# First layer of three batches instead of four in seven products, and all row sums on VectorE

## The chip, the core and the metric

The kernel runs on one core of one Trainium2 chip. The metric is device time in microseconds (us) for one execution, as the median of several runs. TensorE (PE) does the matmuls, VectorE (DVE), ScalarE (ACT) and GpSimd (POOL) the elementwise work, SyncE (SP) only issues DMAs here.[...]

## The reference

Attention without a softmax is followed by a two-layer network with an exact GELU. The outputs of the heads stand side by side as the network's input rows, so that 8 x 448 rows of 768 numbers go through it.

```python
# q, k, v: (8, 12, 448, 64) f32; w_in (768, 2048), w_out (2048, 768)
scores = scale * np.matmul(q, k.transpose(0, 1, 3, 2))      # scale = 1/sqrt(64)
attn = np.maximum(scores, 0.0) ** 2 / S                     # S = 448
attn_out = np.matmul(attn, v)
x = attn_out.transpose(0, 2, 1, 3).reshape(B * S, H * D)    # (3584, 768)
h = x @ w_in
g = 0.5 * h * (1.0 + erf(h * inv_sqrt2))
return g @ w_out
```

## The kernel before, in words

Everything is computed in bf16 with f32 sums. The attention of the eight batches runs one batch after the other, in three groups of four heads. For each group there are seven steps: score matmuls into PSUM (`ps`, L663), a relu with scale from PSUM to the bf16 tile `a_sq` on ACT (L675) or DVE (L677), and its square on DVE (L684, one tile multiplied by itself). When the seven squares of a group are there, the value product (`pav`, L724) follows and is copied to the transposed input `xT` (L440 on DVE or L442 on ACT). Queries and keys have to stand transposed (`qT`, `kT`). From batch 2 on, DMA transposes on SP's queue do this, nine for each batch (L589). POOL issues the loads of the inputs and, between them, small copies called gates (L630), each of which waits for the transposes of a group of heads before the next load overwrites their source.

While the attention of a batch runs, PE takes matmuls of the network in between, from a list called `flow`. The first layer of batches 0 to 3 is computed directly (`add_f1`, `psh`, L776): sixteen blocks of output columns, six matmuls of 448 columns each, and a GELU from PSUM on ACT (L786). The first layer of batches 4 to 7 is computed by `add_blocks`: input, weights and output are each cut into two by two blocks and seven products take the place of eight. It makes 168 matmuls of 224 columns for a batch (`pb`, L924), needs four sums of input blocks on DVE (`xs`, L890), sums of weight blocks (`ws`, L846, once for all batches) and 20 additions on DVE that pass partial results on (`part`, L958). These products come last, after the last score matmul, in the list called `end`; this part is called the tail below.

The second layer is computed for fourteen groups of 256 rows each (`add_group`, `pso`, L1095) by seven products too. The right-hand sums of `w_out` are made once (`t_sb`, L1031). Each group needs four sums of its own rows (`s_sb`, L1075), 128 x 1024 in bf16 each. For groups 2 to 6 these four stand in POOL's queue, placed by the table `POOLED` behind the gates and loads of the batch that it names; for the other groups they are on DVE. After each product DVE or ACT passes the partial result on (L1129, L440, L442), and SP issues the output stores (L1055), in the same queue as the transposes. Groups 1 to 6 stand in `flow` (table `GROUPS`), the later ones in `end`, partly woven with the blocks.

The order of instructions on each engine is written when the program is built. A planner (`Scheduler`) holds a price for each operation (for example 0.69 us for a row sum on DVE, 2.3 on POOL) and places operation after operation; the opening follows a fixed list (`ORDER`), PE's later work follows `pe_q`, POOL's follows `pool_q`. ACT and DVE take what the planner judges due, and a relu can go to either. `F1B` names, for each batch of attention, the batch whose direct first layer is put into `flow`; `SHARES` spreads `flow` over the batches.

Of the kernel before, what the change touches and what calls it, by code (L numbers as in the profile page):

```python
# [12 lines left out]
B, H, S, D = 8, 12, 448, 64  # L13
# [13 lines left out]
KF = FF // 128  # L27
# [27 lines left out]
SUM_BIAS = -0.3  # L55
TSUM_BIAS = 0.2
LEADS = {}
POOLED = {2: 3, 3: 3, 4: 5, 5: 5, 6: 5}
SHARES = (1.3, 1.0, 1.0, 1.0, 1.0, 1.0)
LAST = 256  # L60
PASSES = 5
# [262 lines left out]
def kernel(  # L324
# [9 lines left out]
    nc = tc.nc  # L334
# [101 lines left out]
    V, A = nc.vector, nc.scalar  # L436
# [7 lines left out]
    def e_copy(n, psum=4):  # L444
# [4 lines left out]
    sch = Scheduler({"w": 3, "a": NA, "f": 2, "osb": 3, "s1": 1, "s2": 1, "s3": 1, "s4": 1,  # L449
                     "p": 1})  # L450
    pool_q, pe_q = [], []
# [9 lines left out]
    QK, SQ, AV, X, GL = {}, {}, {}, {}, {}  # L461
    F1, F2 = {}, {}
# [27 lines left out]
    def add_v(b, g0, g1):  # L490
        def fn():
            get_v(b)
            nc.gpsimd.dma_start(vt[b][:, 2 * g0 : 2 * g1], kv_view(v, b, g0, g1))

        old = [o for (bb, *_), o in AV.items() if bb == (b - 2 if b == B - 1 else b - 3)]
        o = dma(fn, (g1 - g0) * 4 * S * 256, old)
        for g in range(g0, g1):
            ld_v[b, g] = [o]

    def add_load(b, g0=0, g1=G):  # L500
        add_k(b, g0, g1)
        add_q(b, g0, g1)
        if b < 3:
            add_v(b, g0, g1)
# [120 lines left out]
    def add_gate(b, g):  # L625


        def fn(e):
            n = (16 * g + 1) * KC
            nc.gpsimd.tensor_copy(gate, get_T(b)[0][:, n : n + 16 * KC : KC])  # L630

        deps = [Tq[b, g, c][0] for c in range(NC)] + [Tk[b, g, 0][0]]
        pool_q.append(sch.add((("POOL", 0.2, 0.3),), fn, deps))
# [174 lines left out]
    def wpart(i, j, m0=0, m1=M1):  # L808
        return win_sb[:, i * K1 : i * K1 + K1, (j * M1 + m0) * 128 : (j * M1 + m1) * 128]
# [19 lines left out]
    def wcols(n, m0, m1):  # L829
        t, m = wtile(n, m0)  # L830
        return t[:, :, 128 * m : 128 * (m + m1 - m0)]

    WS = {}
    blocks = {}

    def add_wsums(after, done):

        last = [o[0] for (bb, *_), o in list(Tq.items()) + list(Tk.items()) if bb == B - 1]
        last += [o for (bb, *_), o in QK.items() if bb == B - 2]
        add, sub = mybir.AluOpType.add, mybir.AluOpType.subtract  # L840

        def one(n, m0, op, a, b, deps):
            m1 = m0 + M1 // 2
            return sch.add(
                (("DVE", 0.95, 1.07),),
                lambda e: V.tensor_tensor(wcols(n, m0, m1), a(m0, m1), b(m0, m1), op=op),  # L846
                deps + last + after,
            )

        def part(i, j):  # L850
            return lambda m0, m1: wpart(i, j, m0, m1)

        def summed(n):
            return lambda m0, m1: wcols(n, m0, m1)

        for m0 in (0, M1 // 2):
            s1 = one(1, m0, add, part(0, 1), part(1, 1), [])
            s2 = one(2, m0, sub, summed(1), part(0, 0), [s1])
            s4 = one(4, m0, sub, part(1, 0), summed(2), [s2])
            s3 = one(3, m0, sub, part(0, 0), part(0, 1), [s1] + done)  # L860
            WS[m0] = {1: s1, 2: s2, 3: s3, 4: s4}

    def add_blocks(b):


        xs = [o for (bb, g, h), v in X.items() if bb == b for o in v]
        box = {}
        add, sub = mybir.AluOpType.add, mybir.AluOpType.subtract
        half = (slice(0, HS), slice(HS, S))

        def x(i, c):
            return lambda: xT[b][:, i * K1 : i * K1 + K1, half[c]]

        def t(n):
            def fn():
                if "t" not in box:
                    tag = "qT" if b == B - 1 else "kT"
                    box["t"] = tpool.tile([128, 4, K1, HS], BF16, tag=tag, name="xs")
                return box["t"][:, n - 1]

            return fn

        gone = [o for (bb, *_), o in QK.items() if bb == (B - 2 if b == B - 4 else B - 1)]
        if b == B - 2:
            gone += blocks[B - 4]

        def xsum(n, op, l, r, deps):
            return sch.add(
                (("DVE", 0.47, 0.58),),
                lambda e: V.tensor_tensor(t(n)(), l(), r(), op=op), deps + xs + gone,  # L890
            )

        t1 = xsum(1, sub, x(0, 1), x(0, 0), [])
        t2 = xsum(2, sub, x(1, 1), t(1), [t1])
        t3 = xsum(3, sub, x(1, 1), x(0, 1), [])
        t4 = xsum(4, sub, x(1, 0), t(2), [t2])
        TS = {1: t1, 2: t2, 3: t3, 4: t4}
        old = readers.get(b - 2, [])
        atoms = []
        for m4 in (0, M1 // 2):  # L900
            bank, todo = {}, []
            for y in range(2):
                ms = range(m4 + 2 * y, m4 + 2 * y + 2)
                todo.append(add_block(b, m4, y, ms, bank, x, t, TS, xs, old, half))
            for p in zip(*todo):
                atoms += [(0.58, o) for o in p]
                blocks.setdefault(b, []).extend(p)
            for name in ("a", "b", "c"):
                u, v = bank["end", name]
                u.joint, v.joint = [v], [u]  # L910
        return atoms
# [143 lines left out]
            queue.pop(0).dma_start(to[k, p0 : p0 + m, c], src[y : y + m, c])  # L1055
            j += m

    def add_group(g, pooled=None):

        rows = [range(256 * g + 128 * x, 256 * g + 128 * x + 128) for x in range(2)]  # L1060
        bs = sorted({r // S for t in rows for r in (t[0], t[-1])})
# [8 lines left out]
        box = {}  # L1070

        def sum_op(n, op, a, b, deps):
            def fn(e):
                box["s", n] = spool.tile([128, K2, 128], BF16, tag=f"s{n}", name=f"s{n}_sb")
                (V if pooled is None else nc.gpsimd).tensor_tensor(box["s", n], a(), b(), op=op)  # L1075

            eng = ("DVE", 0.69, 0.8) if pooled is None else ("POOL", 2.3, 2.5)
            o = sch.add((eng,), fn, deps, need=(f"s{n}",), bias=SUM_BIAS)
            if pooled is not None:
                pooled.append(o)  # L1080
            mine.append(o)
            return o

# [131 lines left out]
    def f1(b):  # L1215
        return [(1.14, add_f1(b, m)) for m in range(KF)]

    def steps(b):
        return [((b, g, i, None),) for g in range(G) for i in range(NK)]
# [54 lines left out]
    def early(eng, get, src, t):  # L1274
        def fn(e):
            get_nat(0)
            copy(e, get(), src)

        n = src.shape[1] * src.shape[2]
        d = 0.07 + n / 960 if eng == "DVE" else 0.12 + 0.00074 * n  # L1280
        return sch.add(((eng, d, d + 0.12),), fn, [landed(t)])

    o = early("ACT", lambda: nq[0][:, :4, : HC * D], q32, 5.3)
# [4 lines left out]
    for eng, i0, i1 in (("DVE", 0, K_CUT), ("ACT", K_CUT, NK)):  # L1288
        c = slice(i0 * D, i1 * D)
        o = early(eng, lambda c=c: nk[0][:, :2, c], k32[:, :, c], 5.45)  # L1290
# [54 lines left out]
    def at(b, n):  # L1345
        return [at_slot(b, n)]
# [1 line left out]
    for g in range(G):  # L1348
        add_load(3, g, g + 1)
    add_v(3, 0, G)  # L1350
    flow, plans, held = [], {}, {}
    F1B = {2: 1, 3: 2, 4: 3}
    GROUPS = {2: (1,), 3: (2, 3), 4: (4, 5), 5: (6,)}
    for b in range(2, B):
        add_steps(steps(b), dve=True)
        if b == 2:
            x1 = f1(1)
            first_atoms = x1[:LEAD]
            flow += x1[LEAD:]
            flow += [(2.6, add_plain(t, n)) for n in (1, 0) for t in (0, 1)]  # L1360
            add_tsums()
        elif b in F1B:
            flow += f1(F1B[b])
        if b + 1 < B:

            n = {2: 2}.get(b, 1)
            add_T_dma(b + 1, [at(b, n + y // 3) for y in range(9)])
            if b + 2 < B:
                for g in range(G):
                    add_gate(b + 1, g)  # L1370
                    add_load(b + 2, g, g + 1)
                add_v(b + 2, 0, G)
        flow += [y for g in GROUPS.get(b, ()) for y in add_group(g, held.setdefault(g, []) if g in POOLED else None)]
        for g in POOLED:
            if g in held and POOLED[g] == b:
                pool_q.extend(held[g])
    add_wsums(at(B - 1, 1), [F1[B - 5, m, None] for m in range(KF)])

    def woven(x, y):


        out, y = [], list(y)
        for n, o in enumerate(x):
            out.append(o)
            if n % 14 in (3, 9):
                out.append(y.pop(0))
        return out + y

    end = list(add_blocks(B - 4))
    end += woven(add_blocks(B - 3), add_group(7))  # L1390
    end += add_group(8)
    end += woven(add_blocks(B - 2), add_group(9))
    g10 = add_group(10)
    end += g10 + woven(add_blocks(B - 1), add_group(11))
    end += add_group(12) + add_group(13)
    pe_q.extend(x[1] for x in first_atoms)
    total, gone, edge = sum(x[0] for x in flow), 0.0, 0.0
# [50 lines left out]
```

## Time and profile before

| | |
|---|---|
| median of 3 runs | 401.08 us (397.18 to 409.08) |
| the profiled execution | 401.08 us, its span 399.3 us |
| PE busy | 366.6 us (92% of the span), 3629 matmuls |
| DVE busy | 305.4 us (76%) |
| ACT busy | 204.3 us (51%) |
| POOL busy | 110.2 us (28%) |
| attention of batches 2 to 7 | from 65.0 to 260.6 us of the span |
| tail, from the last score matmul | 260.6 to 399.3 us |

A stretch is bound by the engine that is busy throughout it. Where no engine is, one looks for the wait that ends last and for what released it. PE's clock is granted in shares, 1.00 being full speed[...]. In lines of the profile, `a<-b,c` names the tile written and the tiles read, and `xN` the number of instructions in the line. Batches, groups of heads and groups of rows are counted from 0.

### The profile page before, as it was taken

The page shows a single profiled execution, that of the slowest core. Times are in us where ns is not written, and L with a number is a line of the kernel's source. Part 1 is how long each engine was busy: PE and PEld are TensorE (multiplying, and loading weights), DVE is VectorE, ACT ScalarE, POOL GpSimd, SP SyncE. Part 2 cuts the span into 40 slices and gives each one's busy share as a digit, 9 for nine tenths or more (in the row PEclk, how much of TensorE's full clock was granted, in tenths as well). Part 3 has the DMA queues.
Part 4 walks back from the last instruction along what each step waited for, and adds up shares of the span by engine and source line. Part 5 has one row for each costly group of instructions (what it writes and reads, how often), then busy time and mean ns, then how long its engine had stood idle before and what let it go on. Part 6 is the DMA issues. An engine that isn't in the chain of part 4 may idle for free.

```text
span 399.3 us, 8659 instructions
## 1 busy us (share of the span) xinstructions
PE 366.6 (92%) x3629; PEld 231.3 (58%) x3629; DVE 305.4 (76%) x484; ACT 204.3 (51%) x316; POOL 110.2 (28%) x123
## 2 busy tenths in 40 slices
PE   8699999999999839799979879899999999999995
PEld 7476554455544315354425434469997698689663
DVE  3999814898987708998799979998979766765862
ACT  5988855755587605347745516655553145025300
POOL 8755212401123096901390817200000000000000
PEclk9999999999999969899989969999999999999999
DMA  9999999999999999599996111100201300220232
GB/s 177 194 204 203 202 172 171 203 196 163 194 222 174 162 161 130 119 178 212 189 207 93 41 39 42 39 2 18 65 2 34 97 30 2 80 79 2 71 88 80
DMA packets 89270, 47.28 MB, mean 118 GB/s; under 512 B 55312, under 2 KB 85776, under 8 KB 89232
## 3 DMA queue, kind: packets, MB, share of 16 engines
q0 software_dynamic: 32912, 22.47, 39.4%
q1 hardware_dynamic: 55952, 23.76, 32.5%
q8 instruction: 28, 0.46, 0.5%
q10 hardware_dynamic: 368, 0.51, 0.3%
q14 instruction: 10, 0.08, 0.1%
HBM read 45.61 MB, written 11.01 MB: 142 GB/s over the span
## 4 chain that ended last, share of the span: by engine, by line
PE 66%; DVE 15%; SPq 6%; ACT 5%; DMA 4%; issue 2%; POOL 2%; DVEq 0%; POOLq 0%; ACTq 0%
PE pso L1095 24%; PE pb L924 14%; PE psh L776 14%; DVE a_sq L684 8%; SPq L589 6%; PE ps L663 6%; PE pav L724 5%; DMA qT<-nq 4%; ACT a_sq L675 4%; DVE part L958 2%; DVE osb L1129 1%; DVE a_sq L677 1%; PE spin L1256 1%; DVE ws L846 1%; POOL s_sb L1075 1%
## 5 line engine op out<-in xcount | busy, mean ns | idle before, releaser
L675 ACT ACTIVATE a_sq<-ps 128x896 bf16<-128x896 f32 x131 | 113.4, 918 | 59.6 <-PE ps L663 59.4
L684 DVE TENSOR_TENSOR a_sq<-a_sq 128x896 bf16<-128x896 bf16 (+1 forms) x169 | 116.8, 733 | 3.0 <-ACT a_sq L675 2.3
L776 PE MATMUL psh<-xT,win_sb 128*128 128x448 bf16 (+1 forms) x420 | 77.9, 339 | 0.0
L1095 PEld LDWEIGHTS <-s_sb 128*128 128x128 bf16 x424 | 41.4, 100 | 40.9 <-issue 9.4
L958 DVE TENSOR_TENSOR part<-pb,part 128x448 f32<-128x448 f32 x80 | 46.1, 620 | 22.2 <-PE pb L924 22.2
L776 PEld LDWEIGHTS <-win_sb 128*128 128x128 bf16 x420 | 39.1, 98 | 36.6 <-issue 9.1
L677 DVE TENSOR_SCALAR a_sq<-ps 128x896 bf16<-128x896 f32 (+1 forms) x38 | 40.8, 1075 | 22.9 <-PE ps L663 22.8
L663 PE MATMUL ps<-qT,kT 64*64 64x448 bf16 (+1 forms) x756 | 48.9, 341 | 5.2 <-ACT a_sq L675 2.0
L1095 PE MATMUL pso<-t_sb,s_sb 128*128 128x384 bf16 x208 | 41.5, 347 | 10.1 <-POOL s_sb L1075 8.4
L724 PE MATMUL pav<-a_sq,v_sb 64*64 64x448 bf16 (+1 forms) x756 | 39.2, 333 | 8.6 <-DVE a_sq L684 7.4
L786 ACT ACTIVATE h_sb<-psh 128x448 bf16<-128x448 f32 x64 | 35.0, 550 | 23.2 <-PE psh L776 23.1
L1095 PEld LDWEIGHTS <-h_sb 128*128 128x128 bf16 x312 | 30.6, 100 | 24.6 <-issue 6.7
L1095 PE MATMUL pso<-wout_sb,h_sb 128*128 128x384 bf16 x208 | 39.8, 336 | 2.3 <-DVE osb L1129 2.3
L967 ACT ACTIVATE h_sb<-part 128x448 bf16<-128x448 f32 x48 | 26.7, 578 | 25.4 <-DVE part L958 25.1
L924 PEld LDWEIGHTS <-win_sb 128*128 128x128 bf16 x384 | 36.9, 98 | 3.1 <-issue 1.1
L1095 PE MATMUL pso<-wout_sb,s_sb 128*128 128x384 bf16 (+2 forms) x216 | 38.1, 320 | 0.1
L1129 DVE TENSOR_TENSOR osb<-pso,p_sb 128x384 f32<-128x384 f32 x39 | 21.6, 554 | 18.9 <-issue 10.1
L663 PEld LDWEIGHTS <-kT 64*64 64x64 bf16 x756 | 18.9, 106 | 27.5 <-issue 18.9
L724 PEld LDWEIGHTS <-v_sb 64*64 64x64 bf16 x756 | 21.8, 107 | 21.7 <-issue 12.6
L1075 POOL TENSOR_TENSOR s_sb<-h_sb 128x1024 bf16<-128x1024 bf16 x10 | 23.5, 2350 | 26.9 <-PE pso L1095 26.8
L630 POOL COPY gate<-qT 128x16 bf16<-128x16 bf16 x15 | 4.0, 267 | 94.5 <-DMA qT<-nq 94.5
L924 PEld LDWEIGHTS <-ws 128*128 128x128 bf16 x288 | 27.6, 98 | 0.4 <-issue 0.4
(62 smaller groups left out, 347.9 us busy)
## 6 DMA issues: line engine op xcount, KB each, us to landing
nk<-in_k_dram POOLq DMA_DIRECT2D x23, 224.0 KB, 6.9
nq<-in_q_dram POOLq DMA_DIRECT2D x21, 224.0 KB, 8.5
v_sb<-in_v_dram POOLq DMA_DIRECT2D x5, 672.0 KB, 12.9
out_dram<-osb SPq DMA_DIRECT2D x8, 336.0 KB, 3.2
v_sb<-in_v_dram POOLq DMA_DIRECT2D x9, 224.0 KB, 8.2
out_dram<-osb SPq DMA_DIRECT2D x7, 288.0 KB, 2.8
out_dram<-osb SPq DMA_DIRECT2D x8, 240.0 KB, 3.1
win_sb<-in_moe_w_in_dram POOLq DMA_DIRECT2D x8, 192.0 KB, 8.5
```

The costliest lines, as they stand in the source:

```text
L663: nc.tensor.matmul(ps[64 * j : 64 * j + 64, e, x * w : x * w + w], kT[r, g, i * 128 + 64 * j : i * 128 + 64 * j + 64], moving, start=True, ...
L675: A.activation(ar, ps, AF.Relu, scale=c_att)
L677: V.tensor_scalar(ar, ps, c_att, 0.0, op0=mybir.AluOpType.mult, op1=mybir.AluOpType.max,)
L684: V.tensor_mul(box["a2"][:, :, :used], ar, ar)
L724: nc.tensor.matmul(pav[0][o2 : o2 + 64, e, :w], vt[b][r, 2 * g + e, bass.ts(i, D)], box["a2"][r, y, o : o + w], start=(i == 0), stop=(i == ...
L776: nc.tensor.matmul(ph[:, x * n : x * n + n], win_sb[:, kd, bass.ts(m + x, 128)], xT[b][:, kd, c], start=(kd == 0), stop=(kd == KD - 1),)
L786: A.activation(h_ring()[:, m : m + nm, o + c.start : o + c.stop], box[0][:, :S].rearrange("p (x n) -> p x n", x=nm), AF.Gelu,)
L924: nc.tensor.matmul(bank[name][:, y, z * HS : z * HS + HS], w[:, k, bass.ts(mm, 128)], right()[:, k], start=first and k == 0 and z == 0, st ...
L958: V.tensor_add(get(to), ps(name), get(other))
L967: A.activation(h_ring()[:, m : m + 2, o + half[c].start : o + half[c].stop], src().rearrange("p (x n) -> p x n", x=2), AF.Gelu,)
L1075: (V if pooled is None else nc.gpsimd).tensor_tensor(box["s", n], a(), b(), op=op)
L1095: nc.tensor.matmul(box[bank][:, n0:n1], left()[:, kf], right()[:, kf, n0:n1], start=bool(need) and kf == 0, stop=kf == K2 - 1, skip_group_ ...
```

## The change

The first layer of batch 4 is computed directly. It stands in `flow` with batch 5 (`F1B`), so its 96 matmuls of 448 columns and its sixteen GELUs fall beside attention. `add_blocks` is called for batches 5, 6 and 7 only, and group 7 is still woven with the blocks of batch 5. The sums of weight blocks, one of which is written over a part of `w_in`, wait for the direct first layer of batch 4 instead of batch 3. `POOLED` is gone: the twenty row sums of groups 2 to 6 are on DVE, priced like the others, and POOL's queue holds only gates and loads. The buffers of `add_blocks` no longer have to wait for a fourth batch. As the planner spreads a longer `flow` over the same batches, the network's matmuls stand at other places among those of attention, and so do the stores in SP's queue. The opening, up to batch 2 of attention, keeps its order.

```diff
-POOLED = {2: 3, 3: 3, 4: 5, 5: 5, 6: 5}
...
-        gone = [o for (bb, *_), o in QK.items() if bb == (B - 2 if b == B - 4 else B - 1)]
-        if b == B - 2:
-            gone += blocks[B - 4]
+        gone = [o for (bb, *_), o in QK.items() if bb == (B - 2 if b == B - 3 else B - 1)]
...
-    def add_group(g, pooled=None):
+    def add_group(g):
...
-                (V if pooled is None else nc.gpsimd).tensor_tensor(box["s", n], a(), b(), op=op)
-
-            eng = ("DVE", 0.69, 0.8) if pooled is None else ("POOL", 2.3, 2.5)
-            o = sch.add((eng,), fn, deps, need=(f"s{n}",), bias=SUM_BIAS)
-            if pooled is not None:
-                pooled.append(o)
+                V.tensor_tensor(box["s", n], a(), b(), op=op)
+
+            o = sch.add(
+                (("DVE", 0.69, 0.8),), fn, deps, need=(f"s{n}",), bias=SUM_BIAS
+            )
...
-    F1B = {2: 1, 3: 2, 4: 3}
+    F1B = {2: 1, 3: 2, 4: 3, 5: 4}
...
-        flow += [y for g in GROUPS.get(b, ()) for y in add_group(g, held.setdefault(g, []) if g in POOLED else None)]
-        for g in POOLED:
-            if g in held and POOLED[g] == b:
-                pool_q.extend(held[g])
-    add_wsums(at(B - 1, 1), [F1[B - 5, m, None] for m in range(KF)])
+        flow += [y for g in GROUPS.get(b, ()) for y in add_group(g)]
+    add_wsums(at(B - 1, 1), [F1[B - 4, m, None] for m in range(KF)])
...
-    end = list(add_blocks(B - 4))
-    end += woven(add_blocks(B - 3), add_group(7))
+    end = woven(add_blocks(B - 3), add_group(7))
     end += add_group(8)
```

More of the change, by code (lines that the diff above doesn't have):

```diff
@@ L833 @@
     WS = {}
-    blocks = {}
     def add_wsums(after, done):
@@ L906, in add_blocks @@
                 atoms += [(0.58, o) for o in p]
-                blocks.setdefault(b, []).extend(p)
             for name in ("a", "b", "c"):
@@ L1350 @@
     add_v(3, 0, G)
-    flow, plans, held = [], {}, {}
-    F1B = {2: 1, 3: 2, 4: 3}
+    flow, plans = [], {}
+    F1B = {2: 1, 3: 2, 4: 3, 5: 4}
     GROUPS = {2: (1,), 3: (2, 3), 4: (4, 5), 5: (6,)}
```

## The prediction

> **What bounds the kernel now.** I first cut the span at the first score matmul of each batch and read the busy time in each stretch; the whole-span shares (PE 92%, DVE 76%) hide that the batches differ. Columns: stretch, its length, then busy time of PE, PE weight loads, DVE, ACT and POOL, the granted clock, the DMA share and GB/s. The rows are the attention of batches 2 to 7, then what follows the last score matmul.
>
> ```profile
> 65.00:97.56 32.56, 31.92 (x278) 16.18 (x278) 28.50 (x42) 21.16 (x31) 5.33 (x8) 1.00 1.31 186
> 97.56:125.53 27.97, 27.08 (x268) 13.86 (x268) 22.94 (x36) 19.28 (x28) 5.84 (x10) 1.00 1.28 197
> 125.53:167.04 41.51, 30.12 (x270) 15.11 (x270) 27.88 (x38) 17.07 (x23) 26.86 (x24) 0.88 1.04 143
> 167.04:194.23 27.19, 27.19 (x269) 13.88 (x268) 23.71 (x39) 17.77 (x25) 5.21 (x10) 1.00 1.28 200
> 194.23:225.81 31.58, 28.80 (x270) 13.94 (x270) 28.58 (x35) 17.45 (x24) 17.43 (x12) 0.95 0.85 131
> 225.81:260.60 34.79, 28.20 (x257) 13.59 (x256) 31.91 (x42) 15.97 (x21) 15.20 (x7) 0.90 0.15 42
> 260.60:399.31 138.71, 133.55 (x1124) 105.40 (x1116) 99.81 (x177) 48.34 (x92) 0.00 (x0) 1.00 0.16 46
> ```
>
> Batches 2, 3 and 5 are PE bound: PE works nearly all the time at full clock. Batches 4, 6 and 7 hold about as many matmuls and take up to 14 us longer, with a lower clock. Those three are the ones with much POOL work. The timeline of batch 4 shows the largest hole (start, length, engine, line, idle before it and its releaser):
>
> ```profile
> 139.25 0.21 POOL L630 COPY gate<-qT 128x16 bf16<-128x16 bf16 x1 [9.24 <-DMA qT<-nq]
> ...
> 142.04 2.13 POOL L1075 TENSOR_TENSOR s_sb<-h_sb 128x1024 bf16<-128x1024 bf16 x1
> 144.26 2.11 POOL L1075 TENSOR_TENSOR s_sb<-s_sb,h_sb 128x1024 bf16<-128x1024 bf16 x1
> ...
> 146.42 2.74 PE L1095 MATMUL pso<-t_sb,s_sb 128*128 128x384 bf16 x8 [8.43 <-POOL s_sb L1075]
> ```
>
> The sums s_sb stand in POOL's queue behind a gate that waits for a transpose; PE waits 8.43 us for the second of them. The other two bad batches have no such hole. There I asked for the squares (L684) alone in the same stretches (length, DVE busy, clock, DMA):
>
> ```profile
> 97.56:125.53 27.97, 12.18 (x21) 1.00 1.28 197
> ...
> 125.53:167.04 41.51, 16.84 (x21) 0.88 1.04 143
> 167.04:194.23 27.19, 12.28 (x22) 1.00 1.28 200
> 194.23:225.81 31.58, 17.50 (x19) 0.95 0.85 131
> 225.81:260.60 34.79, 19.76 (x21) 0.90 0.15 42
> ```
>
> The same squares cost 12.2 us where POOL makes no sums and 16.8, 17.5 and 19.8 where it does. Three squares from 201.58 on take 6.01 us in the timeline beside POOL sums, against 1.69 for three beside none. So the excess is 4.6 + 5.3 + 7.6 = 17.5 us of DVE time, in batches where DVE is busy 28 to 32 us: there it becomes the bound.
>
> [...] The trace shows 0.66 over 140 to 150 us, behind the 8.43 us hole, and 1.00 over both stretches beside it, so that a hole costs a little more than its length.
>
> **The change part by part.** Rates are from the chain of waits, where runs of one kind follow each other:
>
> ```profile
> 182.01 3.51 PE psh L776 x18
> ...
> 290.78 4.60 PE pb L924 x48
> 295.38 1.30 PE pso L1095 x8
> ```
>
> This is 0.195 us per first-layer matmul of 448 columns, 0.0958 per block matmul of 224, 0.163 per second-layer matmul. Scores come to 0.0615 and values to 0.0475 each from the same chain (12 in 0.69 to 0.76, 28 in 1.32).
>
> (1) Batch 4's first layer leaves the seven-product blocks. The tail loses 168 block matmuls, 168 x 0.0958 = 16.1 us. The attention phase gains 96 matmuls, 96 x 0.195 = 18.7 us. PE alone: +2.6 us. Both parts lie on the path, as PE is the bound in the tail and in the good batches.
>
> (2) With the instruction order of the two builds and these rates, PE's own work in batches 2 to 7 is 32.0, 27.3, 26.7, 27.4, 26.6, 23.5 before (163.5; measured 195.6, so 32.1 us lost, 31.1 of it in batches 4, 6 and 7) and 35.9, 30.5, 29.6, 29.6, 30.4, 26.2 after (182.2). The tail's work is 133.4 before (measured 138.7, so 5.3 of ramp and drain) and 117.3 after.
>
> (3) Twenty sums go from POOL (47 us there) to DVE, at 0.684 us each by the 32 that DVE makes already: 13.7 us. POOL's queue keeps gates and loads only, so both the hole and the squares' excess lose their cause. What is late next at 138 us: the third part of batch 4's scores, whose transposes had landed by 139.25 (the gate that waits for them ends there), while their turn comes two thirds into the batch, about 143. That is a cover of some 4 us, and batch 4 now starts about 6 us later on PE.
>
> (4) DVE in the attention phase: before 263.3 - 99.8 = 163.5 us. Less the excess, 146.0. Plus 22 sums (two more come forward from the tail), 15.0. Less 8 relus that the planner gives to ACT, 8 x 1.08 = 8.6. Plus 6 copies of xT from ACT, 3.6. Plus 3 weight sums that come forward, 2.9. Together 159 us of 182, 87%. In batches 2, 3 and 5 DVE was busy 75.15 of 87.72 us, 86%, and cost PE next to nothing. ACT gains 8 relus x 0.92 and 16 gelus x 0.55, less 6 copies, 13 us over six batches that left it about 40% idle: nothing on the path. The 20 fewer adds and 4 fewer block sums in the tail lie beside PE: nothing.
>
> (5) SP and POOL queues. The loads and the nine transposes per batch are the same; output stores stand at other places among them, seven sets among the transposes of batches 5 to 7 where four stood. From one gate to the same gate of the next batch took 28.0 us (97.57 to 125.54), and a batch of PE work is now about 30. So transposes gain on PE: I take zero, and price the contrary below.
>
> The sum: 65.0 up to batch 2 (same order of instructions) + 182.2 + losses + 117.3 + 5.3, plus 1.8 outside the span (401.08 - 399.3; the profiled run is also the median, of 397.18 to 409.08). The good batches lost about 0.5 each, so 3.2. DVE at 86% gives the same, 159 / 0.857 = 185.5. The sums are not spread evenly: batches 4 and 6 get eight and seven, with DVE work near PE's own 30 us. I take 4 us more for these, from bounds of 0 and 13 (the DVE rival). Total 65.0 + 189.4 + 122.6 + 1.8 = **378.8, say 379 us**, 22 below the run before.
>
> **The rivals.**
> - *Nothing lost.* PE runs without a hole: 65.0 + 182.2 + 122.6 + 1.8 = 371.6. For it: batch 5 had none. Against: no six batches in a row did so.
> - *DVE becomes the bound* where the sums are. Batches 6 and 7 of before, with DVE as the bound, reach 90 to 92%. My count of DVE work by batch after is 36, 24, 30, 24, 30, 29; at 91% where it binds and at PE's pace elsewhere this gives 39.6 + 31.2 + 33 + 30.1 + 32.6 + 31.9 = 198.4, and 65 + 198.4 + 122.6 + 1.8 = 388. For it: the sums now stand in the queue in which squares wait, and PE's value products wait for squares. Against: batch 2 before held 31 us of DVE work by the same count and lost 0.6.
> - *The wait only changes its name.* The gate at 139.25 shows that transposes were late too; PE then waits 8.4 us for qT where it waited for s_sb, and some 3 in batch 6: 379 + 11 = 390. Against it, the 143 above.
> - *Slower: stores hold the transposes.* SP issues stores and transposes in one queue; a store that waits for its last add, now behind sums on DVE, holds all transposes behind it, and scores wait for these. The gap from the stores at 162.28 to the next transpose at 168.92 is 6.64 us. Seven sets at 6.64 are 46.5, less some 10 us by which transposes ran ahead, 36.5: 65 + 185.4 + 36.5 + 122.6 + 1.8 = 411. It costs from the point where the waits of a batch exceed that lead. Against: the load for the transpose of 168.92 was issued only at 164.26, so most of that gap was the load's.
>
> **How the numbers follow.** Forecast, with nothing lost as its lower end, 0.65 (372 to 385, at 379); DVE bound 0.17; renamed wait 0.11; stores 0.05; something unseen 0.02. A range of 372 to 391 leaves out about 2 in 10. Two per cent, about what a measurement tells from no change, is 393.1 to 409.1: the first three cases lie below it but for their upper ends, hence 0.86 faster, 0.08 within, 0.06 slower.
>
> **What would show it.** Right: no s_sb on POOL; squares at about 12.2 us in every batch; batches 4, 6 and 7 at 30 to 33, 30 to 33 and 26 to 31 us, clock 1.00 in all; batches 2, 3 and 5 longer by 3 to 4, 3 and 2 to 3 us; the tail at 121 to 125. Wrong: waits of PE for DVE squares of over 10 us in all (DVE rival), waits of scores for qT over 5 us (renamed wait, stores), or a tail that does not shrink by 16.

## The result, and the profile after

The changed kernel takes 372.09 us (371.12 to 372.79, 4 runs) against 401.6 us (397.18 to 409.08, 4 runs): a ratio of 0.930 with a 95% interval of 0.922 to 0.938, faster by 29.5 us. The ratio is that of the fast runs alone, without the slow one of 409.08, so it is not the quotient of the two medians. The forecast was 379 in a range of 372 to 391.

Busy time by stretch of the kernel after, cut like the one before (length, then PE, PE weight loads, DVE, ACT, POOL, granted clock, DMA share, GB/s): batches 2 to 7, then the tail.

```profile
66.69:102.44 35.75, 35.75 (x303) 18.50 (x302) 31.50 (x47) 20.46 (x30) 8.85 (x14) 1.00 1.28 195
102.44:132.53 30.09, 30.09 (x283) 14.95 (x282) 23.31 (x38) 21.56 (x32) 4.29 (x7) 1.00 1.37 176
132.53:162.62 30.09, 30.09 (x291) 15.67 (x290) 27.42 (x49) 18.44 (x23) 7.04 (x12) 1.00 1.29 183
162.62:191.91 29.29, 29.29 (x281) 14.76 (x280) 22.24 (x35) 20.69 (x31) 6.92 (x12) 1.00 1.27 181
191.91:222.73 30.82, 30.69 (x292) 15.86 (x292) 27.07 (x47) 19.72 (x26) 2.53 (x4) 1.00 1.05 173
222.73:249.00 26.27, 26.05 (x259) 13.21 (x262) 24.24 (x40) 19.55 (x28) 0.00 (x0) 1.00 0.01 2
249.00:370.50 121.50, 116.83 (x958) 89.32 (x948) 82.88 (x148) 37.27 (x70) 0.00 (x0) 1.00 0.18 53
```

Every batch is PE bound now, with PE busy (nearly) throughout and the granted clock at 1.00. The six batches take 182.3 us, where PE's own work was reckoned at 182.2; before they took 195.6 for 163.5. The tail went from 138.7 to 121.5.

PE's four largest waits from batch 2 to the last score matmul, before (who waited for whom, us in total, times, longest):

```profile
PE pso L1095 <- POOL s_sb L1075: 8.4, 1, 8.4
PE pav L724 <- DVE a_sq L684: 7.4, 7, 1.9
PE pso L1095 <- DVE osb L1129: 3.9, 3, 2.3
PE ps L663 <- DMA qT<-nq: 1.5, 2, 0.9
```

and the whole of the same answer after:

```profile
PE ps L662 <- ACT a_sq L674: 0.2, 1, 0.2
```

All four are gone, the two waits for transposed queries too. The squares alone (length, DVE busy, clock, DMA share, GB/s), for batches 3 to 6 after:

```profile
102.44:132.53 30.09, 12.17 (x21) 1.00 1.37 176
132.53:162.62 30.09, 12.85 (x21) 1.00 1.29 183
162.62:191.91 29.29, 12.01 (x21) 1.00 1.27 181
191.91:222.73 30.82, 12.60 (x21) 1.00 1.05 173
```

They cost 12 to 13 us in each of these batches. Before it was 16.8 to 19.8 where POOL made sums beside them.

### The profile page after: what moved, and what is told of

It reads as the page before. It is cut to its first block, busy times and chain, and to the rows that moved or that the text cites. A ratio compares the mean times of both kernels' runs of the same rounds, so it can differ in the third digit from the quotient of the medians.

```text
span 370.5 us, 8484 instructions
## 1 busy us (share of the span) xinstructions
PE 359.3 (97%) x3557; PEld 222.1 (60%) x3557; DVE 281.0 (76%) x479; ACT 205.2 (55%) x313; POOL 64.0 (17%) x103
## 4 chain that ended last, share of the span: by engine, by line
PE 91%; ACT 3%; DMA 1%; DVE 1%; issue 1%; POOL 1%; DVEq 0%; POOLq 0%; ACTq 0%
PE pso L1089 31%; PE psh L775 25%; PE pb L919 13%; PE ps L662 9%; PE pav L723 8%; PE pso L1184 3%; ACT a_sq L674 2%; DMA nq<-in_q_dram 1%; PE tp L561 1%; DVE part L953 1%; POOL nk L474 0%; PE tp L533 0%; DVE xs L886 0%; ACT kT L441 0%; DVE osb L1123 0%
## 5 line engine op out<-in xcount | busy, mean ns | idle before, releaser
L674 ACT ACTIVATE a_sq<-ps 128x896 bf16<-128x896 f32 x139 | 120.0, 918 | 31.1 <-PE ps L662 30.9
L683 DVE TENSOR_TENSOR a_sq<-a_sq 128x896 bf16<-128x896 bf16 (+1 forms) x169 | 98.4, 617 | 5.8 <-ACT a_sq L674 4.7
L775 PE MATMUL psh<-xT,win_sb 128*128 128x448 bf16 (+1 forms) x516 | 96.3, 340 | 0.0
L785 ACT ACTIVATE h_sb<-psh 128x448 bf16<-128x448 f32 x80 | 43.8, 549 | 29.6 <-PE psh L775 29.6
L1089 PEld LDWEIGHTS <-s_sb 128*128 128x128 bf16 x424 | 40.4, 98 | 27.4 <-issue 3.3
L953 DVE TENSOR_TENSOR part<-pb,part 128x448 f32<-128x448 f32 x60 | 34.6, 620 | 21.5 <-PE pb L919 21.5
L676 DVE TENSOR_SCALAR a_sq<-ps 128x896 bf16<-128x896 f32 (+1 forms) x30 | 32.1, 1074 | 24.7 <-PE ps L662 24.5
L1089 PE MATMUL pso<-t_sb,s_sb 128*128 128x384 bf16 x208 | 38.1, 326 | 0.0
L962 ACT ACTIVATE h_sb<-part 128x448 bf16<-128x448 f32 x36 | 20.1, 578 | 20.2 <-DVE part L953 20.0
L439 DVE CAST xT<-pav 128x448 bf16<-128x448 f32 (+1 forms) x45 | 24.4, 582 | 8.5 <-PE pav L723 8.4
L919 PEld LDWEIGHTS <-ws 128*128 128x128 bf16 x216 | 20.7, 98 | 0.0
```

Of the source, the lines that this page charges most:

```text
L439: V.tensor_copy(dst, src)
L674: A.activation(ar, ps, AF.Relu, scale=c_att)
L676: V.tensor_scalar(ar, ps, c_att, 0.0, op0=mybir.AluOpType.mult, op1=mybir.AluOpType.max,)
L683: V.tensor_mul(box["a2"][:, :, :used], ar, ar)
L775: nc.tensor.matmul(ph[:, x * n : x * n + n], win_sb[:, kd, bass.ts(m + x, 128)], xT[b][:, kd, c], start=(kd == 0), stop=(kd == KD - 1),)
L785: A.activation(h_ring()[:, m : m + nm, o + c.start : o + c.stop], box[0][:, :S].rearrange("p (x n) -> p x n", x=nm), AF.Gelu,)
```

## The experiments

My theory was that the POOL sums made all of the 32 us that batches 2 to 7 lost, by a wait behind a gate and by the stretched squares. The rivals were that the wait only changes its name, and that the shift of batch 4's first layer made the gain.

### Each part alone

The sums alone: `add_blocks` stays at four batches.

```diff
-POOLED = {2: 3, 3: 3, 4: 5, 5: 5, 6: 5}
+POOLED = {}
```

> The kernel before with one part of the change alone: the twenty row sums on DVE, the first layer of batches 4 to 7 still in seven products. My theory (the POOL sums made the whole loss, by the wait behind the gate and by stretched squares; the shift of batch 4's layer costs PE 2.6 us and gives DVE cover): nearly all the gain comes back, but DVE now holds about 160 us of work beside 163.5 us of PE work in batches 2 to 7, so it binds in places: 374 to 382 us. Rival 1 (the layer shift is pure cost, DVE never binds): 369 to 371, faster than the changed kernel. Rival 2 (the layer shift made the gain): 390 us or more.

Measured: 381.24 us (381.1 to 383.21), ratio 0.945 (0.939 to 0.950). So the sums alone bring 22 of some 30 us. The time is in the theory's range, but not for its reason: in the one bad batch, batch 5, DVE was busy 25.6 of 34.3 us, and the wait there was another (further below). One caution: this edit of one line makes the planner lay out the rest anew, so that 154 of the 3629 matmuls stand at another place in PE's order than before.

The layer alone: `F1B`, the weight sums and `end` as in the change, the sums left on POOL. With the sums at their old places in POOL's queue, the planner comes to a point at which no operation can start. So their places are moved as well, and each group's sums are planned behind the work of the group before (`prior`); the comparison is not of the layer quite alone.

```diff
-POOLED = {2: 3, 3: 3, 4: 5, 5: 5, 6: 5}
+POOLED = {2: 2, 3: 3, 4: 4, 5: 4, 6: 5}
...
-    F1B = {2: 1, 3: 2, 4: 3}
+    F1B = {2: 1, 3: 2, 4: 3, 5: 4}
...
+                o.deps += prior.get(g - 1, [])
                 pooled.append(o)
...
-    end = list(add_blocks(B - 4))
-    end += woven(add_blocks(B - 3), add_group(7))
+    end = woven(add_blocks(B - 3), add_group(7))
```

> The kernel before with the layer part alone: batch 4's first layer computed directly beside the attention of batch 5, the twenty row sums still on POOL (those of group 2 behind the loads issued in batch 2, of group 3 in batch 3, of groups 4 and 5 in batch 4, of group 6 in batch 5, since PE's new order asks for them earlier; each group's sums are planned behind the products of the group before). Theory: the POOL sums still stretch squares by about 17 us; the POOL reads that nobody waits for cost the changed kernel 13 us, and waits behind gates come on top: 384 to 398 us. Rival (the layer shift made the gain by itself): 372 to 376.

Measured: 397.14 us (393.38 to 399.61), ratio 0.985 (0.974 to 0.997): the layer alone is worth some 6 us. No PE wait for POOL's results is left in this run, and yet it is 25 us above the changed kernel. The squares of its batches 3 to 6 cost 81.5 us for 85 of them, where the changed kernel needs 49.6 for 84. Its timeline of batch 3 shows how that reaches PE (start, length, engine, line, idle before and releaser):

```profile
114.31 10.55 DVE L684 TENSOR_TENSOR a_sq<-a_sq 128x896 bf16<-128x896 bf16 x3
115.09 4.23 POOL L1075 TENSOR_TENSOR s_sb<-h_sb 128x1024 bf16<-128x1024 bf16 x2
119.26 2.13 POOL L1075 TENSOR_TENSOR s_sb<-s_sb,h_sb 128x1024 bf16<-128x1024 bf16 x1
121.47 2.39 POOL L1075 TENSOR_TENSOR s_sb<-h_sb,s_sb 128x1024 bf16<-128x1024 bf16 x1
...
125.92 0.59 PE L663 MATMUL ps<-qT,kT 64*64 64x448 bf16 x4 [4.48 <-DVE a_sq L677]
```

Three squares last 10.55 us: the first 7.57, until three of POOL's sums are through, the others beside and behind the fourth. The relu behind them (124.79 us) frees its PSUM buffer late, and PE waits 4.48 us.

### The hole without the stretching, the stretching without the hole

First the hole alone is taken away: group 2's sums stand ahead of the gates.

```diff
-POOLED = {2: 3, 3: 3, 4: 5, 5: 5, 6: 5}
+POOLED = {2: 2, 3: 3, 4: 5, 5: 5, 6: 5}
...
+                o.deps += prior.get(g - 1, [])
                 pooled.append(o)
```

> The kernel before with the sums of group 2 put into POOL's queue ahead of the gates of batch 4 instead of behind them; everything else stays, sums on POOL included. It takes the hole of 8.4 us away but not the stretched squares. Theory: the hole and the slow clock behind it are worth 9 to 12 us, so 389 to 393 us, the squares of batches 6 and 7 still at 17 to 20 us. Rival (the wait only changes its name: PE then waits for transposed queries at the same place): 398 to 402, with a wait of score matmuls for qT of over 5 us in batch 4.

Measured: 402.11 us, ratio 0.997 (0.993 to 1.000): next to nothing, and a miss for the theory as put. The rival named about the right time for a wrong reason, since no wait for qT stands among PE's waits, of which these are the largest:

```profile
PE ps L663 <- DVE xT L440: 6.6, 2, 4.5
PE pav L724 <- DVE a_sq L684: 5.4, 4, 1.9
```

The 8.4 us wait for POOL is gone; 1.3 us of waits for `s_sb` is left. Batch 4 falls from 41.5 to 31.7 us, and its granted clock rises from 0.88 to 0.96 (the prediction's 0.66 is the clock granted from 140 to 150 us in the kernel before). But group 2's sums now run beside the squares of batch 3, which rise from 12.2 to 17.9 us, while the batch grows from 28.0 to 33.3 (its squares: length, DVE busy, clock, DMA share, GB/s):

```profile
98.28:131.59 33.31, 17.86 (x21) 0.95 1.30 169
```

In the kernel before, these sums ran while PE stood still and DVE had nothing to do for 10.1 us, so they stretched few squares. With 1.3 us more in batch 7, most of the 9.8 us won in batch 4 came back. The hole was one form in which POOL's sums were paid, and a free queue mostly changed it into the other. (The planner moved other DVE work along with the sums, so that not every us of this has one cause.)

Next the stretching alone is put back: POOL additions in the changed kernel that nobody waits for.

```diff
+        for _ in range({3: 8, 5: 12}.get(b, 0)):
+            pool_q.append(sch.add((("POOL", 2.3, 2.5),), extra, []))
...
+    def extra(e):
+        for kd in range(4):
+            nc.gpsimd.tensor_tensor(
+                junk, win_sb[:, kd, :256], win_sb[:, kd, 256:512], op=mybir.AluOpType.add
+            )
```

> The changed kernel with 80 additions of 128x256 on POOL that nobody waits for: 32 behind the loads issued in batch 3, 48 behind those issued in batch 5; they read the first-layer weights and write a scratch tile. Only the contention of POOL reads with DVE squares is put back, no wait of PE for POOL. Theory: squares beside these additions take two to three times as long, 10 to 18 us of DVE time in all, of which DVE's idle time hides a half or more: 375 to 384 us. Rival (the stretched squares of the kernel before cost nothing, only waits for POOL results did): 371 to 373, or squares that stay at 0.62 us.

And the control, in which POOL is held but reads nothing:

```diff
-        for kd in range(4):
-            nc.gpsimd.tensor_tensor(
-                junk, win_sb[:, kd, :256], win_sb[:, kd, 256:512], op=mybir.AluOpType.add
-            )
+        for _ in range(8):
+            nc.gpsimd.memset(junk, 0.0)
```

> The changed kernel with 160 memsets of 128x256 on POOL that nobody waits for, at the places where the additions of the run before last stood (64 behind the loads issued in batch 3, 96 behind those issued in batch 5). They hold POOL's queue for some tens of us, and so the gates and loads behind them, but read nothing. Theory (reads of POOL against squares are the cost): 371 to 374 us, squares at about 12.2 us in a batch. Rival (POOL's queue being held, so that loads come late, is the cost of the 385 us): 380 us or more.

Measured: 384.99 us (384.22 to 385.74) with the additions, 372.4 us (371.13 to 372.71) with the memsets. In the traces, PE, DVE and ACT do the same work in the same order in both runs as in the changed kernel, so nothing but POOL's extra work differs. The additions held POOL for 31 and 49 us, the memsets for 24 and 35. In both runs the first block lies in front of gates and loads of a later batch, the second behind the last of them. Late loads are not the cause: with the additions no wait for qT stands among PE's waits, and batch 7, which grew most (26.3 us in the changed kernel), lies beside the second block, behind which no load stands. POOL additions that read SBUF cost 12.9 us, memsets that only write it 0.3: I take the reads as the cause. DVE's busy time in the whole span rose by 21.6 us, from the first of these lines (the changed kernel) to the second (with the additions):

```profile
PE 359.3 (97%) x3557; PEld 222.1 (60%) x3557; DVE 281.0 (76%) x479; ACT 205.2 (55%) x313; POOL 64.0 (17%) x103
PE 361.8 (94%) x3557; PEld 221.4 (58%) x3557; DVE 302.6 (79%) x479; ACT 205.4 (54%) x313; POOL 137.7 (36%) x183
```

Some 15 us of it are squares (98.4 us became 113.7). Among the rest are row sums, whose two inputs are in SBUF too: in these lines (busy us, then the mean of one in ns; again the changed kernel, then the additions) one grows from 682 to 767 ns. In the kernel before, a sum of weight blocks took 1.95 us beside POOL's sums (at 246.07 us) and 0.96 without. DVE instructions with an input in PSUM kept their length there: beside POOL's sums relus took 1.07 to 1.09 us (at 200.57, 207.52 and 224.29 us), against a mean of 1.09 in the changed kernel, and additions to `osb` 0.54 and 0.55 (at 161.71 and 245.14), against 0.56.

```profile
L1070 DVE TENSOR_TENSOR s_sb<-h_sb 128x1024 bf16<-128x1024 bf16 x26 | 17.7, 682 | 0.0
L1070 DVE TENSOR_TENSOR s_sb<-h_sb 128x1024 bf16<-128x1024 bf16 x26 | 19.9, 767 | 0.0
```

Of the 21.6 us the time shows 12.9, so some 40% was hidden, not far from the half or more that was expected. The cost stands mostly where DVE becomes the bound, in batch 7 (with the additions; length, then PE, PE weight loads, DVE, ACT, POOL):

```profile
226.20:261.60 35.40, 28.84 (x263) 13.56 (x262) 35.33 (x42) 19.86 (x28) 30.34 (x32) 0.95 0.12 30
```

Here DVE has no pause left, and the batch is 9.1 us longer than in the changed kernel. Batch 4, with DVE busy 30.8 of 31.4 us, is longer by only 1.3. The squares' durations over the whole run (shortest, median, longest in ns), with the additions and with the memsets:

```profile
L683 DVE TENSOR_TENSOR a_sq<-a_sq x169: 387/620/1089, 8.4 to 264.2; 128x896 bf16<-128x896 bf16 x167, 128x448 bf16<-128x448 bf16 x2
```

```profile
L683 DVE TENSOR_TENSOR a_sq<-a_sq x169: 386/618/639, 8.3 to 251.4; 128x896 bf16<-128x896 bf16 x167, 128x448 bf16<-128x448 bf16 x2
```

With the memsets none is stretched (the longest 0.64 us, 0.63 in the changed kernel), and DVE is busy 281.0 us again.

### How near DVE is to being the bound

```diff
-                V.tensor_tensor(box["s", n], a(), b(), op=op)
+                for _ in range(2 if 2 <= g <= 6 else 1):
+                    V.tensor_tensor(box["s", n], a(), b(), op=op)
```

> The changed kernel with each of the twenty row sums of groups 2 to 6 made twice on DVE, one after the other, 13.7 us more DVE work between batches 2 and 7; the result is the same. It measures how far DVE is from being the bound. If DVE binds from about 91% busy, as the forecast's rival had it: 378 to 385 us. If DVE's idle time still holds this work: 372 to 375 us.

Measured: 377.32 us (376.53 to 380.02), between the two expectations: 13.7 us of DVE work cost 5.2. PE and ACT keep their order. Batch 6, which got more of the added work than any other, in the view by stretch:

```profile
194.50:226.90 32.40, 31.23 (x291) 15.89 (x291) 31.76 (x55) 19.83 (x26) 0.84 (x1) 1.00 0.74 136
```

DVE is busy 31.76 of 32.40 us, 98%, and the batch is only 1.6 us longer than in the changed kernel. So 91% is not where DVE begins to bind. Nor is 98% a ceiling to be carried elsewhere: batches 3 and 5 grew by 1.3 and 2.2 us with DVE busy 82% and 78% of them. At the start of batch 5 a relu stands behind two doubled sums, and PE waits 1.6 us for it. What a sum costs depends on what stands behind it in DVE's queue, and the share of a whole batch does not tell that.

### What the sums alone still lost

Between the sums alone and the changed kernel lie 9 us, though the layer shift gives PE 2.6 us more to do. In the run of the sums alone, DVE's wait in batch 5, and what PE waited for:

```profile
DVE osb L1129 <- DMA out_dram<-osb: 6.8, 1, 6.8
...
PE pso L1095 <- DVE osb L1129: 5.4, 1, 5.4
PE ps L663 <- DMA qT<-nq: 2.0, 2, 1.7
```

An addition needs an output buffer that is not stored yet. The store stands behind transposes in SP's queue: DVE's last write to `osb` ended at 156.09 us, the store was issued from 159.53 on (start, length; the eight stores issued from 159.5 to 171.4 us landed 4.3 to 10.6 us later):

```profile
151.21 3.47 SPq L589 DMA_TRANSPOSE kT<-nk  x1
154.74 4.68 SPq L589 DMA_TRANSPOSE qT<-nq  x2
159.53 2.32 SPq L1055 DMA_DIRECT2D out_dram<-osb  x4
```

I tried to take the stores of groups 1 to 6 out of that queue, on top of the sums alone:

```diff
+            eng, q = (("ACT", 0.9, 3.0), nc.scalar) if g <= 6 else (("SP", 0.6, 2.8), nc.sync)
+            sch.add((eng,), store(1, full, [q] * 2), [c22, c21], frees=("osb",))
+            sch.add((eng,), store(0, full, [q] * 2), [c11] + c12, frees=("osb",))
```

> The kernel before with the twenty row sums on DVE (as in the run of the sums alone, 381.2 us) and, beside that, the output stores of groups 1 to 6 issued from ACT's queue instead of SP's, where transposes stand ahead of them. In the run of the sums alone PE lost 5.4 us at 166 us to a DVE add that waited 6.8 us for an output buffer not yet stored. Theory: that wait goes, 374 to 377 us. Rival (DVE's load makes the rest of the difference to the changed kernel): 379 to 382 us.

Measured: 390.75 us (388.0 to 393.0), 9.5 more than with the stores on SP: a miss on both sides. The wait for the buffer is gone, but relus on ACT now wait for transposes; that answer for ACT:

```profile
ACT a_sq L675 <- DMA qT<-nq: 13.1, 2, 9.6
```

ACT issued a store, at 115.82 us, just ahead of the relu of 117.40, before which it stood idle for 9.59 us; SP had issued transposes of qT from 110.46 us on. That the store was what waited for a transpose, with the relu behind it, is my reading and not shown. The run doesn't decide the question. Leaving out the stores of groups 2 to 6, so that their output is not written, does:

```diff
+                fn = store(x, full, [nc.sync] * 2) if g > 6 or g == 1 else lambda e: None
```

> The kernel before with the twenty row sums on DVE (the run of the sums alone, 381.2 us), with the output stores of groups 2 to 6 left out: 1280 of the 3584 rows are not written. PE does the same work, so what goes is the cost of these stores in SP's queue and in the DMA engines. Theory (without the layer shift a batch of PE work is 27 us while transposes take 28, and stores stuck between transposes hold output buffers): the wait of 5.4 us at 166 us goes and nothing comes instead: 372 to 376 us. Rival (DVE's load, or PE's own order, makes the 9 us between the sums alone and the changed kernel): 378 to 382 us.

Measured: 374.43 us (373.18 to 375.3). In the traces PE, DVE and ACT do the same work in the same order as in the run of the sums alone, and batch 5 falls from 34.3 to 27.4 us (first the sums alone, then without these stores):

```profile
153.50:187.80 34.30, 28.90 (x273) 14.16 (x272) 25.59 (x44) 19.81 (x28) 7.55 (x13) 0.95 1.29 201
154.40:181.80 27.40, 27.40 (x269) 13.69 (x268) 25.53 (x44) 19.79 (x28) 7.18 (x12) 1.00 1.35 163
```

DVE is as busy there as in the run of the sums alone (25.53 against 25.59 us), so its load was not the cause; the stores were. Last, all stores stay, and the planner's price for a transpose is changed, which moves the stores in SP's queue:

```diff
-T_STEP = 1.4
+T_STEP = 2.6
```

> The kernel before with the twenty row sums on DVE, planned with a price of 2.6 us instead of 1.4 for a transpose in SP's queue, near the 28 us that nine of them took per batch. All outputs are written; only the order in the queues changes, stores standing further ahead among the transposes. If stores behind transposes are what the sums alone still lost: 371 to 377 us, where the changed kernel is at 372. If not: 379 to 383.

```diff
-T_STEP = 1.4
+T_STEP = 3.1
```

> The same with a price of 3.1 us, which moves more stores ahead of transposes. If stores behind transposes are what the sums alone still lost: 371 to 377 us. If stores ahead of transposes hold the transposes (the forecast's slower rival): 380 us or more, with scores waiting for qT.

Measured: 375.22 us (372.62 to 377.36; ratio 0.935, 0.927 to 0.942) at 2.6, and 384.63 us (384.11 to 386.64) at 3.1. The first has no wait for output buffers or qT and comes close to the changed kernel (0.930, 0.922 to 0.938), so the layer shift is not needed for most of the gain. That the stores' new places brought this is likely but not shown: the price moves more than stores, and 194 of the 3629 matmuls stand at another place in PE's order than with the sums alone, with other orders on DVE and ACT too. The second is slower, but without the waits for qT that the stores rival calls for: its six batches are longer than in the first by 2.4, 2.6, 1.5, 3.5, 1.3 and 1.0 us, and its longest PE waits, for ACT and DVE, are 0.8 to 1.4 us. Which step of its order costs that, no run separates. No version tried is faster than the changed kernel.

## Why the prediction was right

Its mechanism and direction held, and the time is that of its case in which nothing is lost (371.6), not of its own 379. That it lies in the range, 0.1 us above the lower end, has luck in it: two small terms that it took as fixed added 2.1 us (the last point below). The single terms:

- *PE's work* (steps 1 and 2). Reckoned 182.2 and measured 182.3 us for batches 2 to 7; the tail 122.6 and 121.5.
- *The sums leave POOL* (step 3). Right, and confirmed from two sides: the sums alone bring 22 us, POOL reads alone cost 13. Its split was wrong: the hole is hardly a separate part. Without it (402.11) the same sums are paid for the most part as stretched squares. Its 17.5 us of excess counted 21 squares in each batch; batch 6 has 19, which makes it 18.7.
- *DVE's work* (step 4). Reckoned 159 us, measured 238.65 - 82.88 = 155.8, 85% of 182.3.
- *Losses*, 3.2 + 4 us in the sum. This is the mis-sized term: they measured 0.1. The 3.2 came from the 0.5 us that each good batch had lost (six times 0.5 is 3.0), and all of this was waits for qT. With 30 us of PE work in a batch against 28 of transposes such waits were not to be expected, and none came; step 5 had said so ("transposes gain on PE"), and the sum did not use it. The 4 came between 0 and the 13 of the DVE rival, and this 13 was too large for two reasons. Its counts of DVE work by batch (36, 24, 30, 24, 30, 29) add up to 173 us, against the 159 of step 4; measured were 31.5, 23.3, 27.4, 22.2, 27.1 and 24.2. With these, even 91% as the bound would cost about 1 us by the same working (27.4 and 24.2 over 0.91 against PE's 29.6 and 26.2), not 16. And the 91% was read from batches in which the squares themselves were stretched; such a batch has waits in DVE's own chain and says nothing of what DVE can hold. Batch 7 after has DVE busy 24.24 of 26.27 us, 92%, and PE 26.05.
- *The signs*. All that were named came but one: batch 3 grew by 2.1 us, not by 3.
- *The rest*: the opening ended 1.7 us later (66.7 instead of 65.0; the other runs, with the same opening, show 65.1 to 66.8), and 2.2 us lie outside the span instead of 1.8 (372.69 - 370.5 for the profiled run). 378.8 - 7.1 - 1.1 + 1.7 + 0.4 = 372.7.

The stores rival did not occur in the changed kernel, but it was near in the run of the sums alone, and in the reverse form: not stores that hold transposes, which the prediction assumed and no run shows, but transposes that hold stores, and through them output buffers (6.8 us, the wait at 165.51 us). In the changed kernel that wait is absent. Batches of PE work that are longer than the transposes take (30 us against 28, without the layer shift 27) would explain it, but so would the order that came with the shift: the first is argued from these figures and not shown.

## What to carry to other kernels

Moving work to POOL is not free merely because POOL is idle (before, it was busy 28% of the span, and moving its twenty sums to DVE brought 22 us): ask what DVE runs meanwhile, and compare one DVE group's time in stretches with and without POOL work before trusting shares of the span. When you price such a contention, count every DVE instruction of the kind that is slowed, not only the largest group (the squares were some 15 of 21.6 us here). Read what an engine can hold only from stretches in which its instructions have their undisturbed durations (here 91% for DVE was read from stretched ones, and 98% was measured in a batch without POOL's sums), and see that the counts by stretch add up to the total. Where stores and transposes share a queue, shortening the compute of a batch to less than its transposes take (27 us against 28 here) may bring up waits that were covered before; here this is argued, not shown.

## What was not expected of the hardware

The prediction's sample was three squares in 6.01 us, some 2.0 each, beside POOL sums of 2.1 to 2.5 us. In the run of the layer alone one square lasted longer than three sums took: 7.57 us, from 114.31 us on. The sums from 115.09 to 121.39 took 4.23 us for the first two and 2.13 for the third, as the sums of the kernel before did while DVE stood idle (2.11 to 2.13), so they lost nothing to the square. The fourth sum, begun at 121.47, took 2.39. In the run without the hole the longest square took 4.58 us, in the kernel before 2.54. Why the two get in each other's way, what decides which of them is held, and what held this square in the 0.8 us ahead of the first sum, no run shows. With four shorter additions in place of each sum (0.93 us by the median, x80) the longest square was 1.09 us. The squares' excess over the changed kernel was 15 us there, for 80 us of POOL reads, and 18 us in the kernel before, for 47.
